# An attention and PReLU MLP kernel: batch 0's remainder rows move to the GpSimd queue, and the first two blocks of the MLP are put in another order

## The chip, the cores and the metric

The kernel runs on one core of one Trainium2 chip. The metric is device time in microseconds (us) of that core. Engines are named as in the profile: PE is TensorE's matmul, PEld its weight load, DVE is VectorE, ACT is ScalarE, POOL is GpSimd, SP is SyncE. SP, ACT and POOL each also issue DMAs on a queue of their own.

## The reference

For 8 batches and 8 heads, with S = 576 tokens and 64 columns a head, the attention has no softmax; its output, with heads side by side, is the input x (4608 x 512) of a two-layer MLP with a PReLU between.

```python
kv  = einsum('bhsd,bhse->bhde', k, v)
out = einsum('bhsd,bhde->bhse', q, kv)
x   = out / sqrt(mean(out*out, axis=-1) + 1e-6) * g_norm   # -> (4608, 512)
h   = x @ w_in                                             # (4608, 2048)
y   = (maximum(h, 0) + alpha * minimum(h, 0)) @ w_out      # (4608, 512)
```

## The kernel before

**Stages.** The 4608 tokens are cut into nine blocks of 512 (w = 0 to 8). A block's x needs the attention of the batch or two that it overlaps. While block w runs its first MLP product (16 "units" u = 0 to 15, each an `m1_group` of four matmuls into one PSUM bank), the same loop (lines 680 to 709) also runs the second product of block w-1 and the attention steps of block w+1. Block 0 is different: its first product stands alone (lines 575 to 587), its second product is written as four ordinary tiles `ys[0..3]` of 16 matmuls each (`y_run`, `y_mm`, line 353; the argument g = 0 to 15 is the depth slice), and block 1's attention is woven between them by hand (lines 598 to 640). From the second product of block 1 on (line 476, `prod_mm`), a seven-product scheme with 112 half-width matmuls a block is used; it needs sums of weights (`w_sum`) and of activations (`s_sum`), both on DVE. The prediction calls lines 598 to 640 the hand-woven part, and the loop's passes w = 1 and w = 2 loop stage 1 and loop stage 2.

**Order.** Every engine runs its instructions in the order in which the code emits them (`manual_schedule`). So a place in the code is a place in the queue of each engine that the step uses.

**The head.** Each batch has 512 "main" rows and 64 remainder rows a head. For batch 0, SP and ACT load the fp32 remainders of q, k and v into `rem0` tiles (`early_rem`, line 76) and the fp32 first four heads of q and k (`early_half`, line 82); `cast_rem` (line 534) and `cast_pair` (line 528) convert them to fp16 on DVE and ACT. POOL's queue, which converts while it loads, brings the other halves (`load_main`, line 142), then the weights and the later batches (`load_rem` line 148, `load_main`). A POOL load reuses the semaphore of the load eight places ahead of it, and waits for that one to land.

**Attention steps of a pair of heads j.** `step_t` (five transposes of q, then a copy out of PSUM, on ACT from batch 1 on, line 258), `step_kv` (five matmuls, then a masked copy on DVE, line 272), `step_ot` (line 286, squares on ACT, line 292), `ssq_mm` (line 302, `rstd` on ACT, line 304) and `norm` (`xt` on DVE, line 312). `regroup` (line 159) and `regroup_pair` (line 157) bring a batch's q and k from the staging tile into the layout of the matmuls.

**A unit.** `m1_group` takes the next PSUM bank from `h_tags`, four matmuls fill it (line 328), ACT makes `m_sb` (line 335), DVE makes `gt` from `m_sb` and the bank (line 339); only then is the bank free. In loop stage 1 there are two banks, h1 and h2, since h0 and y still hold the open tiles 2 and 3.

```python
def h_bank(name="h_ps"):
    tags = h_tags[0]
    h_turn[0] = (h_turn[0] + 1) % len(tags)
    return ps_h.tile([P, W], FP32, name=name, tag=tags[h_turn[0]])
```

PSUM banks: h0, h1, h2, y, s, q and two o (`ot`). The loop's second product takes y, h0 and q for its three accumulators.

Of the kernel before, what the change touches and what calls it, by code (L numbers as in the profile page):

```python
# [9 lines left out]
FP32 = mybir.dt.float32  # L10
# [7 lines left out]
def kernel(  # L18
# [17 lines left out]
    P = 128  # L36
    NPAIR = H // 2
# [3 lines left out]
    TPP = S // P  # L41
# [26 lines left out]
    )  # L68

    srcs = {"q": q, "k": k, "v": v}  # L70
    rem0 = {}
    st32 = {}

    def early_rem(eng, nm):
        rem0[nm] = ysb_p.tile([P, H, D], FP32, name=f"rem0{nm}", tag="y_sb")
        eng.dma_start(
            out=rem0[nm][0:REM], in_=srcs[nm][0, :, MAIN:S, :].rearrange("h s d -> s h d"),
        )

    def early_half(eng, nm, tag):  # L80
        st32[nm] = w_p.tile([P, H // 2, TPP * D], FP32, name=f"{nm}32", tag=tag)
# [2 lines left out]
            in_=srcs[nm][0, 0 : H // 2, 0:MAIN, :].rearrange("h (p t) d -> p h (t d)", t=TPP),  # L84
        )

    early_rem(nc.sync, "q")
    early_rem(nc.scalar, "k")
    early_half(nc.sync, "q", "wsum2")
    early_half(nc.scalar, "k", "wsum4")  # L90
    early_rem(nc.sync, "v")

    _set_id = list(get_activation_tables(nc.m.arch).keys()).index(
        "abs_reciprocal_sqrt_and_small"
# [32 lines left out]
    bufs = []  # L127
# [9 lines left out]
    def load_main(b, nm, h0, h1):  # L137
        st = stages.get((b, nm))
        if st is None:
            st = stage_p.tile([P, H, TPP, D], FP16, name=f"{nm}st", tag=f"{nm}st")  # L140
            stages[b, nm] = st
        nc.gpsimd.dma_start(  # L142
            out=st[:, h0:h1, :, :].rearrange("p h t d -> p h (t d)"),
            in_=srcs[nm][b, h0:h1, 0:MAIN, :].rearrange("h (p t) d -> p h (t d)", t=TPP),
        )

    def load_rem(b, nm):
        nc.gpsimd.dma_start(
            out=bufs[b % NBUF][nm][0:REM, 0 if nm == "v" else TPP, :, :],
            in_=srcs[nm][b, :, MAIN:S, :].rearrange("h s d -> s h d"),  # L150
        )
# [14 lines left out]
    def regroup_pair(b, nm, j):  # L166
        regroup(b, nm, 2 * j, 2 * j + 2, nc.scalar)
# [32 lines left out]
        return w_out_sb[i][:, r, :]  # L200

    HH = H // 2
    load_main(0, "v", 0, HH)
    load_main(0, "q", HH, H)
    load_main(0, "k", HH, H)
    ident = const_p.tile([P, P], FP32, name="ident")
    make_identity(nc, ident[:])
    load_main(0, "v", HH, H)
    for i in range(len(IN_CUTS) - 1):
        load_w_in(i)  # L210
# [184 lines left out]
    def w_sum(n, i):  # L395
        sl = slice(i * GW, (i + 1) * GW)
        if n not in wsum:
            wsum[n] = w_p.tile([P, NK, HC], FP16, name=f"wsum{n}", tag=f"wsum{n}")
        if n == 1:
            nc.vector.tensor_sub(  # L400
                out=wsum[1][:, sl, :], in0=w_lo(i, HC, D_MODEL), in1=w_lo(i, 0, HC)
            )
        elif n == 2:
            nc.vector.tensor_sub(
                out=wsum[2][:, sl, :], in0=w_hi(i, HC, D_MODEL), in1=wsum[1][:, sl, :]
            )
        elif n == 4:
            nc.vector.tensor_sub(
                out=wsum[4][:, sl, :], in0=w_hi(i, 0, HC), in1=wsum[2][:, sl, :]
            )  # L410
        else:
            nc.vector.tensor_sub(
                out=wsum[3][:, sl, :], in0=w_hi(i, HC, D_MODEL), in1=w_lo(i, HC, D_MODEL),
            )
# [115 lines left out]
            in_=st[:, 2 * j : 2 * j + 2, :].rearrange("p h (t d) -> p h t d", t=TPP),  # L530
        )

    def cast_rem(nm, eng_copy):
        eng_copy(out=bufs[0][nm][0:REM, 0 if nm == "v" else TPP, :, :], in_=rem0[nm][0:REM])

    cast_pair("q", st32["q"], 0, nc.vector.tensor_copy)
    cast_rem("q", nc.vector.tensor_copy)
    cast_pair("k", st32["k"], 0, nc.scalar.copy)
    cast_rem("k", nc.scalar.copy)
    step_t(0, 0, H_POOL)  # L540
    cast_pair("q", st32["q"], 1, nc.vector.tensor_copy)
# [52 lines left out]
    def y_run(a, gs):  # L594
        for g in gs:
            y_mm(ys[a], 0, a, g)
# [4 lines left out]
    w_sum(1, 0)  # L601
    for j, pool in enumerate((S_POOL, Q_POOL, O_POOL, O_POOL)):
        step_t(1, j, pool)
    for a in (0, 1):
        y_run(a, range(4, 8))
    y_run(2, (4, 5))
    w_sum(1, 1)
    step_kv(1, 0)
    step_kv(1, 1, Q_POOL)
# [4 lines left out]
    y_run(3, (6,))  # L614
    step_ot(1, 1)
    y_run(3, (7,))
    ssq_mm(1, 0)
    norm(1, 0)
    y_run(0, (8, 9))
    ssq_mm(1, 1, Q_POOL)  # L620
    norm(1, 1)
    y_run(0, (10, 11))
    step_ot(1, 2)
    w_sum(2, 0)
    y_run(1, (8, 9))
    step_ot(1, 3)
    w_sum(4, 0)
    y_run(1, (10, 11))
    ssq_mm(1, 2)
    norm(1, 2)  # L630
    y_run(0, (12, 13))
    ssq_mm(1, 3, Q_POOL)
    norm(1, 3)
    y_run(0, (14, 15))
    y_out(ys[0], 0, 0)
    w_sum(2, 1)
    y_run(1, range(12, 16))
    y_out(ys[1], 0, 1)
    w_sum(4, 1)
    w_sum(3, 0)  # L640
    h_tags[0] = ("h1", "h2")
    h_turn[0] = 1
    LATER = [(2, 6), (2, 7)] + [(2 + i % 2, 8 + i // 2) for i in range(2 * (NF - 8))]

    S_AT = {
# [6 lines left out]
    def unit_sums(w, u):  # L652
        for back, n, k in S_AT.get(u, ()):
            if 1 <= w + back < NW:
                s_sum(w + back, n, k)
# [4 lines left out]
            ATT_AT.setdefault(3 * j + at, []).append((what, j))  # L660
    ATT_1 = {}
    for what, ats in (
        ("kv", (3, 4, 5, 6)), ("t", (6, 7, 8, 9)), ("ot", (8, 9, 11, 12)), ("ssq", (10, 11, 13, 14))
    ):
        for j, at in enumerate(ats):
            ATT_1.setdefault(at, []).append((what, j))
    ATT = {"t": step_t, "kv": step_kv, "ot": step_ot, "ssq": step_ssq}

    def attention(w, u):
        if w < NW:  # L670
            for what, j in (ATT_1 if w == 2 else ATT_AT).get(u, ()):
                if w < B or what in ("ot", "ssq"):
                    if w == 2 and what in ("kv", "ssq"):
                        (step_kv if what == "kv" else step_ssq)(w, j, Q_POOL)
                    else:
                        ATT[what](w, j)

    REG_AT = {8 + 2 * j + i: ((nm, j),) for j in range(NPAIR) for i, nm in ((0, "q"), (1, "k"))}

    for w in range(1, NW):  # L680
        if w + 2 < B:
            load_batch(w + 2)
        for u in range(NF):
            m1_group(w, G_ORDER[u])
            unit_sums(w, u)
            if w == 1 and u == 1:
                w_sum(3, 1)
            if w == 1 and u in (2, 5):
                regroup(2, "k" if u == 2 else "q", 0, H)
            if w == 1 and u == 14:  # L690
                regroup(3, "k", 0, H)
            if w > 2 and u == 0:
                y_read(w - 2, "c12")
            if w == 1:
                for _ in range(2 if u < 2 else 1):
                    a, g = LATER.pop(0)
                    y_mm(ys[a], 0, a, g)
                    if g == NF - 1:
                        y_out(ys[a], 0, a)
            else:  # L700
                for i in range(u * PER, (u + 1) * PER):
                    prod_mm(w - 1, *Y_LIST[i])
                for what in Y_READS.get(u, ()):
                    y_read(w - 1, what)
            attention(w + 1, u)
            if w + 2 < B:
                for nm, j in REG_AT.get(u, ()):
                    if w > 1 or nm == "q":
                        regroup_pair(w + 2, nm, j)
    w = NW - 1  # L710
    store_engines[0] = (nc.sync, nc.scalar)
    for u in range(NF):
# [40 lines left out]
```

## Time and profile before

| | us |
|---|---|
| median of 3 runs | 306.36 |
| runs | 305.97 to 308.59 |
| the profiled execution, its own time | 306.55 |
| span of the profile in that execution | 304.8 |

The page's engine totals over the span are PE 281.4 us (92%), DVE 222.2 (73%), ACT 175.4 (58%), POOL 43.6 (14%). A PE total near the span does not say that PE is limiting everywhere: matmuls overlap, and their ends are modelled, so gaps between issues are larger than the idle time that is shown. The rows below go by stretch of time.

### The profile page before, as it was taken

How to read it: one execution, taken by the hardware profiler on the slowest of the kernel's cores; microseconds unless marked ns; L12 is line 12 of the kernel's file. 1: busy time of each engine (PE TensorE's matmuls, PEld its weight loads, DVE VectorE, ACT ScalarE, POOL GpSimd, SP SyncE). 2: the span in 40 equal slices, each digit the busy share in tenths (PEclk: the TensorE clock that was granted, in tenths of full speed). 3: DMA queues.
4: the chain of work that ended last, by engine and by line, in shares of the span. 5: the costliest groups of instructions: out<-in, count | busy, mean ns of one | idle time of the engine just before them, and what ended most of it. 6: DMA issues, size and time to landing. Idle time of an engine off the chain costs nothing.

```text
span 304.8 us, 5163 instructions
## 1 busy us (share of the span) xinstructions
PE 281.4 (92%) x1970; PEld 179.7 (59%) x1970; DVE 222.2 (73%) x421; ACT 175.4 (58%) x305; POOL 43.6 (14%) x61
## 2 busy tenths in 40 slices
PE   4379999897899999999999999999999999999993
PEld 1144454353476667676766676666666666666682
DVE  4256856876767887788778877887788788877861
ACT  1246736468856875687578757875664565443210
POOL 8344345240200420042003000000000000000000
PEclk9579999999999999999999999999999999999998
DMA  7999999999260398139812910021102010201223
GB/s 140 219 205 197 198 201 191 217 183 142 75 73 19 54 182 121 29 48 188 112 34 28 188 38 21 17 70 36 37 0 71 34 36 12 74 19 35 69 76 100
DMA packets 53081, 28.86 MB, mean 95 GB/s; under 512 B 15152, under 2 KB 52544, under 8 KB 53056
## 3 DMA queue, kind: packets, MB, share of 16 engines
q0 software_dynamic: 39792, 17.63, 46.2%
q1 hardware_dynamic: 11424, 9.58, 11.0%
q10 hardware_dynamic: 1840, 1.31, 1.5%
q8 instruction: 15, 0.25, 0.3%
q14 instruction: 10, 0.08, 0.1%
HBM read 36.71 MB, written 9.44 MB: 151 GB/s over the span
## 4 chain that ended last, share of the span: by engine, by line
PE 75%; DVE 10%; ACT 7%; DMA 3%; issue 3%; SPq 0%; DVEq 0%; ACTq 0%
PE h_ps L328 33%; PE yY L476 12%; PE yZ L476 10%; PE yX L476 9%; DMA q<-in_q_dram 3%; PE qt_ps L246 3%; PE kv_ps L264 3%; DVE gt L339 3%; ACT m_sb L335 3%; DVE xt L312 2%; PE ot_ps L286 2%; PE ssq_ps L302 2%; PE y L353 2%; ACT rstd L304 1%; DVE y_sb L503 1%
## 5 line engine op out<-in xcount | busy, mean ns | idle before, releaser
L328 PE MATMUL h_ps<-xt,w_in_sb 128*128 128x512 f16 x576 | 145.8, 379 | 2.1 <-DVE gt L339 1.4
L339 DVE SCALAR_TENSOR_TENSOR gt<-m_sb,beta_sb,h_ps 128x512 f16<-128x512 f32 x144 | 107.2, 747 | 51.7 <-ACT m_sb L335 49.9
L335 ACT ACTIVATE m_sb<-h_ps 128x512 f32<-128x512 f32 x144 | 86.1, 599 | 69.2 <-PE h_ps L328 53.6
L328 PEld LDWEIGHTS <-w_in_sb 128*128 128x128 f16 x576 | 54.2, 98 | 47.6 <-issue 3.8
L476 PEld LDWEIGHTS <-s 128*128 128x128 f16 x512 | 50.1, 98 | 21.6 <-issue 2.5
L476 PEld LDWEIGHTS <-gt 128*128 128x128 f16 x384 | 37.6, 98 | 15.4 <-issue 0.7
L476 PE MATMUL yY<-wsum,s 128*128 128x256 f16 x256 | 36.3, 273 | 0.0
L476 PE MATMUL yX<-w_out_sb,gt 128*128 128x256 f16 x256 | 35.1, 272 | 0.0
L292 ACT ACTIVATE sq_sb<-ot_ps 128x512 f16<-128x512 f32 x36 | 21.3, 598 | 16.8 <-PE ot_ps L286 16.4
L312 DVE SCALAR_TENSOR_TENSOR xt<-ot_ps,g2col,rstd 128x512 f16<-128x512 f32 x36 | 26.5, 746 | 5.2 <-ACT rstd L304 5.0
L304 ACT ACTIVATE rstd<-ssq_ps,eps_t 128x512 f32<-128x512 f32 x36 | 24.4, 688 | 9.8 <-PE ssq_ps L302 9.8
L258 ACT COPY qt_sb<-qt_ps 128x576 f16<-128x576 f16 x28 | 17.5, 638 | 6.4 <-PE qt_ps L246 6.4
L246 PE MATMUL qt_ps<-ident,qsb 128*128 128x128 f16 x160 | 14.5, 230 | 7.0 <-DVE qsb L528 7.0
L476 PE MATMUL yZ<-w_out_sb,s 128*128 128x256 f16 x128 | 17.5, 272 | 1.2 <-DVE y_sb L503 1.2
L353 PE MATMUL y<-w_out_sb,gt 128*128 128x512 f16 x64 | 18.4, 379 | 0.1
L142 POOL DMA_DIRECT2D vst<-in_v_dram x9 | 7.8, 869 | 68.3 <-PE kv_ps L264 62.1
L476 PE MATMUL yZ<-wsum,s 128*128 128x256 f16 x128 | 17.6, 273 | 0.0
L476 PE MATMUL yY<-wsum,gt 128*128 128x256 f16 x128 | 17.6, 273 | 0.0
L246 PEld LDWEIGHTS <-qsb 128*128 128x128 f16 x160 | 11.5, 103 | 9.8 <-DVE qsb L528 7.8
L286 PE MATMUL ot_ps<-qt_sb,kv_sb 128*128 128x512 f16 (+7 forms) x64 | 13.9, 293 | 2.6 <-DVE xt L312 2.2
L264 PEld LDWEIGHTS <-ksb 128*128 128x128 f16 x160 | 11.7, 101 | 5.6 <-issue 2.5
L264 PE MATMUL kv_ps<-vst,ksb 128*128 128x128 f16 x128 | 12.4, 224 | 2.4 <-ACT rstd L304 1.0
(60 smaller groups left out, 223.8 us busy)
## 6 DMA issues: line engine op xcount, KB each, us to landing
out_dram<-y_sb SPq DMA_DIRECT2D x72, 64.0 KB, 2.2
kst<-in_k_dram POOLq DMA_DIRECT2D x7, 512.0 KB, 9.4
qst<-in_q_dram POOLq DMA_DIRECT2D x7, 512.0 KB, 8.7
vst<-in_v_dram POOLq DMA_DIRECT2D x7, 512.0 KB, 7.1
out_dram<-y_sb SPq DMA_DIRECT2D x23, 128.0 KB, 2.1
w_out_sb<-in_moe_w_out_dram POOLq DMA_DIRECT2D x4, 512.0 KB, 16.3
w_in_sb<-in_moe_w_in_dram POOLq DMA_DIRECT2D x3, 512.0 KB, 16.1
out_dram<-y_sb SPq DMA_DIRECT2D x4, 256.0 KB, 5.2
```

The source lines that it names most:

```text
L246: nc.tensor.matmul(out=qt_ps[:, t * P : (t + 1) * P], lhsT=qs(t), rhs=ident16[:], is_transpose=True, start=(t == 0), stop=(t == NT - 1),)
L258: nc.scalar.copy(out=qts[b, j][:], in_=qt_ps[:, 0:S])
L264: nc.tensor.matmul(out=kv_ps[:], lhsT=ks(t), rhs=vs(t), start=(t == 0), stop=(t == NT - 1),)
L286: nc.tensor.matmul(out=ot_ps[:, n0 - w * W : n1 - w * W], lhsT=kvs[b, j][:], rhs=qts[b, j][:, n0 - b * S : n1 - b * S], start=True, stop=True,
L292: nc.scalar.activation(out=sq[:], in_=ot_ps[:], func=AF.Square)
L304: nc.scalar.activation(out=rstd[:], in_=ssq_ps[:], func=AF.Abs_reciprocal_sqrt, bias=eps_t[:], scale=inv_d,)
L312: nc.vector.scalar_tensor_tensor(out=xts[w, j][:], in0=ot_ps[:], scalar=g2col[:], in1=rstd[:], op0=ALU.mult, op1=ALU.mult,)
L328: nc.tensor.matmul(out=h_ps[:], lhsT=w_in_blk(c, g), rhs=xts[w, c][:], start=(c == 0), stop=(c == NC - 1),)
L335: nc.scalar.activation(out=m_sb[:], in_=h_ps[:], func=AF.Relu, scale=-1.0)
L339: nc.vector.scalar_tensor_tensor(out=gts[w, i][:, r, :], in0=m_sb[:], scalar=beta_sb[:, g : g + 1], in1=h_ps[:], op0=ALU.mult, op1=ALU.add,)
L353: nc.tensor.matmul(out=y[:], lhsT=gt_cols(w, g, a * P, (a + 1) * P), rhs=w_out_blk(g), start=(g == 0), stop=(g == NF - 1),)
L476: nc.tensor.matmul(out=bank, lhsT=lhs, rhs=rhs, start=fresh, stop=(c == NK - 1), skip_group_check=True,)
```

## The change

1. `early_rem`, `cast_rem` and the `rem0` tiles are gone. SP's and ACT's queues begin with the fp32 halves of q and k. POOL's queue begins with the three remainders of batch 0 (`load_rem(0, ...)`), converted while they load; `ident` is made ahead of the last half of k.
2. In the hand-woven part, tiles 2, 0 and 1 are all finished (48 matmuls, with the 8 of tile 3 that stood there already); before, tiles 0 and 1 were. Weight sums and batch 2's k copy move ahead of the loop.
3. In loop stage 1 only the last 8 matmuls of tile 3 are left, and h_tags has three banks until the first unit of loop stage 2 has taken its bank.
4. Attention steps of block 2 take other units and, in part, other banks: kv alternates q and o, the third `ot` takes y. Copies of batch 3's q move to units 12 to 15; its k moves from one DVE copy to four ACT copies in units 0 and 1 of loop stage 2. The first `s_sum`s move by a unit.

```diff
-    early_rem(nc.sync, "q")
-    early_rem(nc.scalar, "k")
     early_half(nc.sync, "q", "wsum2")
     early_half(nc.scalar, "k", "wsum4")
-    early_rem(nc.sync, "v")
...
     HH = H // 2
+    for nm in ("q", "k", "v"):
+        load_rem(0, nm)
     load_main(0, "v", 0, HH)
     load_main(0, "q", HH, H)
-    load_main(0, "k", HH, H)
     ident = const_p.tile([P, P], FP32, name="ident")
     make_identity(nc, ident[:])
+    load_main(0, "k", HH, H)
...
-    for a in (0, 1):
+    for a in (2, 0, 1):
         y_run(a, range(4, 8))
-    y_run(2, (4, 5))
...
+    y_run(2, (8,))
     ssq_mm(1, 0)
     norm(1, 0)
-    y_run(0, (8, 9))
+    y_run(2, (9, 10))
     ssq_mm(1, 1, Q_POOL)
     norm(1, 1)
-    y_run(0, (10, 11))
+    w_sum(2, 0)
+    w_sum(4, 0)
+    y_run(2, (11,))
+    y_run(0, (8, 9, 10))
     step_ot(1, 2)
...
     norm(1, 3)
-    y_run(0, (14, 15))
+    regroup(2, "k", 0, H)
+    w_sum(4, 1)
+    w_sum(3, 0)
+    w_sum(3, 1)
+    y_run(0, (13, 14, 15))
     y_out(ys[0], 0, 0)
-    w_sum(2, 1)
+    y_run(2, range(12, 16))
+    y_out(ys[2], 0, 2)
     y_run(1, range(12, 16))
     y_out(ys[1], 0, 1)
...
-    h_tags[0] = ("h1", "h2")
-    h_turn[0] = 1
+    h_turn[0] = 0
+    h_tags[0] = ("h0", "h1", "h2")
...
-        ("kv", (3, 4, 5, 6)), ("t", (6, 7, 8, 9)), ("ot", (8, 9, 11, 12)), ("ssq", (10, 11, 13, 14))
+        ("kv", (1, 2, 3, 4)), ("t", (5, 6, 7, 9)), ("ot", (7, 8, 10, 11)), ("ssq", (9, 10, 12, 13))
...
+                        pool = O_POOL if what == "kv" and j % 2 else Q_POOL
+                    elif w == 2 and what == "ot" and j == 2:
+                        step_ot(w, j, (ps_y, "y"))
...
+    REG_1 = {12 + j: (("q", j),) for j in range(NPAIR)}
...
+            if w == 1 and u == 4:
+                regroup(2, "q", 0, H)
+            if w == 2 and u == 0:
+                h_tags[0] = ("h1", "h2")
...
+            if w == 2 and u < 2:
+                for j in (2 * u, 2 * u + 1):
+                    regroup_pair(3, "k", j)
```

POOL's queue at the start, before. vst, qst and kst are the staging tiles of v, q and k; the shapes are partitions x heads x elements.

```order
L142 DMA vst<-in_v_dram 128x4x256
L142 DMA qst<-in_q_dram 128x4x256
L142 DMA kst<-in_k_dram 128x4x256
masks.py:197 MEMSET ident 128x128
masks.py:199 ISA
masks.py:199 AFFINE_SELECT ident<-ident 128x128
L142 DMA vst<-in_v_dram 128x4x256
L180 DMA w_in_sb_158<-in_moe_w_in_dram 128x4x256
```

POOL's queue at the same place after the change; qsb, ksb and vsb are the fp16 tiles that the matmuls read.

```order
L138 DMA qsb_126<-in_q_dram 64x8x64
L138 DMA ksb_122<-in_k_dram 64x8x64
L138 DMA vsb_124<-in_v_dram 64x8x64
L132 DMA vst<-in_v_dram 128x4x256
L132 DMA qst<-in_q_dram 128x4x256
masks.py:197 MEMSET ident 128x128
masks.py:199 ISA
masks.py:199 AFFINE_SELECT ident<-ident 128x128
L132 DMA kst<-in_k_dram 128x4x256
L132 DMA vst<-in_v_dram 128x4x256
L170 DMA w_in_sb_155<-in_moe_w_in_dram 128x4x256
```

Three loads now stand ahead of all others on POOL's queue, and every later load is three places further back.

DVE's queue from the third and fourth `norm` of block 1 into loop stage 1, before (wsum are the weight sums, ksb_140 is batch 2's k).

```order
L312 SCALAR_TENSOR_TENSOR xt<-ot_ps,g2col,rstd 128x512 x2
L404 TENSOR_TENSOR wsum_598<-w_out_sb_183,wsum_486 128x1024
L408 TENSOR_TENSOR wsum_607<-w_out_sb_183,wsum_598 128x1024
L412 TENSOR_TENSOR wsum_639<-w_out_sb_181,w_out_sb_171 128x1024
L339 SCALAR_TENSOR_TENSOR gt<-m_sb,beta_sb,h_ps 128x512 x2
L412 TENSOR_TENSOR wsum_639<-w_out_sb_183,w_out_sb_176 128x1024
L339 SCALAR_TENSOR_TENSOR gt<-m_sb,beta_sb,h_ps 128x512
L159 COPY ksb_140<-kst 128x8x4x64
```

The same place after; batch 2's k is ksb_134 here.

```order
L304 SCALAR_TENSOR_TENSOR xt<-ot_ps,g2col,rstd 128x512 x2
L149 COPY ksb_134<-kst 128x8x4x64
L400 TENSOR_TENSOR wsum_590<-w_out_sb_180,wsum_588 128x1024
L404 TENSOR_TENSOR wsum_627<-w_out_sb_178,w_out_sb_168 128x1024
L404 TENSOR_TENSOR wsum_627<-w_out_sb_180,w_out_sb_173 128x1024
L331 SCALAR_TENSOR_TENSOR gt<-m_sb,beta_sb,h_ps 128x512 x2
L264 TENSOR_TENSOR kv_sb<-kv_ps,mask_109 128x128
```

The copy of batch 2's k has moved from behind the third `gt` of loop stage 1 to ahead of the first, and no weight sum is left between `gt`s.

ACT's queue at the end of loop stage 1 and the start of loop stage 2 after the change (qsb_126 and ksb_122 are batch 3's q and k).

```order
L296 ACTIVATE rstd<-ssq_ps,eps_t 128x512
L147 COPY qsb_126<-qst 128x2x4x64
L327 ACTIVATE m_sb<-h_ps 128x512
L147 COPY qsb_126<-qst 128x2x4x64
L327 ACTIVATE m_sb<-h_ps 128x512
L147 COPY qsb_126<-qst 128x2x4x64
L327 ACTIVATE m_sb<-h_ps 128x512
L250 COPY qt_sb<-qt_ps 128x576
L147 COPY ksb_122<-kst 128x2x4x64 x2
L327 ACTIVATE m_sb<-h_ps 128x512
L147 COPY ksb_122<-kst 128x2x4x64 x2
L327 ACTIVATE m_sb<-h_ps 128x512
```

The four q copies now stand in the last four units, and four k copies have come in behind them.

## Rows read from the trace of the kernel before

**Rows 1.** The page: its first line, and DMA's busy tenths in 40 slices.
```profile
span 304.8 us, 5163 instructions
DMA  7999999999260398139812910021102010201223
```
**Rows 2.** Windows by stretch: us, PE, PEld, DVE, ACT, POOL busy (instructions), clock, DMA share, GB/s.
```profile
0.00:12.00 12.00, 3.68 (x10) 1.23 (x10) 4.23 (x18) 2.17 (x3) 7.52 (x15) 0.85 0.92 176
12.00:24.65 12.65, 9.43 (x56) 5.34 (x57) 6.38 (x17) 6.11 (x11) 5.38 (x7) 0.74 1.35 201
38.00:53.40 15.40, 14.74 (x100) 7.59 (x98) 8.71 (x16) 8.10 (x15) 7.44 (x10) 1.00 1.48 196
53.40:83.00 29.60, 25.05 (x152) 12.51 (x151) 22.13 (x39) 19.84 (x36) 6.75 (x9) 1.00 1.13 157
83.00:113.50 30.50, 30.25 (x232) 20.62 (x230) 23.50 (x45) 21.43 (x38) 4.09 (x6) 1.00 0.60 81
```
**Rows 3.** Timeline of the head: start us, us, engine, line, operation [idle before, releaser].
```profile
0.74 0.76 SPq L76 DMA_DIRECT2D rem0q<-in_q_dram  x1
1.56 0.85 SPq L82 DMA_DIRECT2D q<-in_q_dram  x1
...
11.53 0.43 DVE L528 CAST qsb<-q 128x512 f16<-128x512 f32 x1 [6.51 <-DMA q<-in_q_dram]
...
12.01 0.71 PE L246 MATMUL qt_ps<-ident,qsb 128*128 128x128 f16 x5 [6.12 <-DVE qsb L528]
...
13.70 0.62 ACT L534 CAST vsb<-rem0v 64x512 f16<-64x512 f32 x1 [0.93 <-DMA rem0v<-in_v_dram]
...
15.66 0.58 PE L264 MATMUL kv_ps<-vst,ksb 128*128 128x128 f16 x4
```
**Rows 4.** DMA queues from 5 to 9 us (packets, MB), and q's issue (KB, us to landing).
```profile
q0 software_dynamic: 430, 0.21, 40.9%
q1 hardware_dynamic: 383, 0.39, 36.0%
q10 hardware_dynamic: 434, 0.44, 35.5%
...
q<-in_q_dram SPq DMA_DIRECT2D x1, 512.0 KB, 9.9
```
**Rows 5.** Timeline of POOL's queue: what each issue waited for.
```profile
35.21 0.69 POOL L148 DMA_DIRECT2D vsb<-in_v_dram  x1 [1.93 <-DMA qst<-in_q_dram]
...
40.79 0.88 POOL L142 DMA_DIRECT2D qst<-in_q_dram  x1 [1.12 <-DMA vst<-in_v_dram]
...
49.21 0.88 POOL L142 DMA_DIRECT2D vst<-in_v_dram  x1 [1.50 <-PE ssq_ps L302]
```
**Rows 6.** Waits of PE from 53.4 to 83 us: total us, times, longest.
```profile
PE ot_ps L286 <- DVE xt L312: 1.7, 2, 0.9
PE h_ps L328 <- DVE gt L339: 1.1, 2, 0.9
PE kv_ps L264 <- DVE ksb L159: 0.8, 1, 0.8
PE h_ps L328 <- DVE xt L312: 0.5, 1, 0.5
```
**Rows 7.** Timeline of PE in the hand-woven part.
```profile
49.66 0.38 PE L286 MATMUL ot_ps<-qt_sb,kv_sb 128*128 128x64 f16 x2 [0.48 <-DVE xt L312]
```
**Rows 8.** Windows, columns as in rows 2: late in loop stage 1.
```profile
70.00:80.00 10.00, 7.90 (x37) 3.35 (x36) 7.40 (x13) 8.91 (x18) 0.00 (x0) 1.00 0.72 83
```
**Rows 9.** The chain of waits: start us, us that the piece adds, what.
```profile
42.00 1.12 PE qt_ps L246 x20
43.11 2.16 PE y L353 x10
...
83.14 0.86 PE h_ps L328 x4
84.00 0.76 PE yX L476 x7
```
**Rows 10.** Windows, columns as in rows 2: the clock around PE's first pause.
```profile
8.00:10.00 2.00, 0.00 (x0) 0.00 (x0) 0.00 (x0) 0.00 (x0) 0.50 (x1) 0.60 1.23 271
10.00:18.00 8.00, 5.05 (x29) 2.97 (x30) 2.92 (x8) 2.89 (x6) 3.30 (x5) 0.50 1.41 197
18.00:20.00 2.00, 1.45 (x12) 1.02 (x11) 1.41 (x4) 1.40 (x3) 0.88 (x1) 0.84 1.23 205
```

More of the change, by code (lines that the diff above doesn't have):

```diff
@@ L70 @@
     srcs = {"q": q, "k": k, "v": v}
-    rem0 = {}
     st32 = {}
[L74 to L78, printed above, removed]
     def early_half(eng, nm, tag):
@@ L531, in cast_pair @@
         )
-    def cast_rem(nm, eng_copy):
-        eng_copy(out=bufs[0][nm][0:REM, 0 if nm == "v" else TPP, :, :], in_=rem0[nm][0:REM])
     cast_pair("q", st32["q"], 0, nc.vector.tensor_copy)
-    cast_rem("q", nc.vector.tensor_copy)
     cast_pair("k", st32["k"], 0, nc.scalar.copy)
-    cast_rem("k", nc.scalar.copy)
     step_t(0, 0, H_POOL)
@@ L542 @@
     cast_pair("k", st32["k"], 1, nc.scalar.copy)
-    cast_rem("v", nc.scalar.copy)
     step_t(0, 1, H_POOL)
@@ L616 @@
     y_run(3, (7,))
+    y_run(2, (8,))
     ssq_mm(1, 0)
     norm(1, 0)
-    y_run(0, (8, 9))
+    y_run(2, (9, 10))
     ssq_mm(1, 1, Q_POOL)
     norm(1, 1)
-    y_run(0, (10, 11))
+    w_sum(2, 0)
+    w_sum(4, 0)
+    y_run(2, (11,))
+    y_run(0, (8, 9, 10))
     step_ot(1, 2)
-    w_sum(2, 0)
-    y_run(1, (8, 9))
+    y_run(0, (11,))
+    y_run(1, (8,))
     step_ot(1, 3)
-    w_sum(4, 0)
-    y_run(1, (10, 11))
+    y_run(1, (9, 10))
     ssq_mm(1, 2)
+    w_sum(2, 1)
     norm(1, 2)
-    y_run(0, (12, 13))
+    y_run(1, (11,))
+    y_run(0, (12,))
     ssq_mm(1, 3, Q_POOL)
     norm(1, 3)
-    y_run(0, (14, 15))
+    regroup(2, "k", 0, H)
[3 more added lines that the diff above has]
+    y_run(0, (13, 14, 15))
     y_out(ys[0], 0, 0)
-    w_sum(2, 1)
+    y_run(2, range(12, 16))
+    y_out(ys[2], 0, 2)
     y_run(1, range(12, 16))
     y_out(ys[1], 0, 1)
-    w_sum(4, 1)
-    w_sum(3, 0)
-    h_tags[0] = ("h1", "h2")
-    h_turn[0] = 1
-    LATER = [(2, 6), (2, 7)] + [(2 + i % 2, 8 + i // 2) for i in range(2 * (NF - 8))]
+    h_turn[0] = 0
+    h_tags[0] = ("h0", "h1", "h2")
     S_AT = {
@@ L673, in attention @@
                     if w == 2 and what in ("kv", "ssq"):
-                        (step_kv if what == "kv" else step_ssq)(w, j, Q_POOL)
+                        pool = O_POOL if what == "kv" and j % 2 else Q_POOL
+                        (step_kv if what == "kv" else step_ssq)(w, j, pool)
+                    elif w == 2 and what == "ot" and j == 2:
+                        step_ot(w, j, (ps_y, "y"))
                     else:
                         ATT[what](w, j)
+    REG_1 = {12 + j: (("q", j),) for j in range(NPAIR)}
     REG_AT = {8 + 2 * j + i: ((nm, j),) for j in range(NPAIR) for i, nm in ((0, "q"), (1, "k"))}
@@ L684 @@
             m1_group(w, G_ORDER[u])
[L685 to L691, printed above, removed]
+            if w > 1:
+                unit_sums(w, u)
+            if w == 1 and u == 4:
+                regroup(2, "q", 0, H)
+            if w == 2 and u == 0:
+                h_tags[0] = ("h1", "h2")
             if w > 2 and u == 0:
@@ L694 @@
             if w == 1:
[L695 to L699, printed above, removed]
+                if u < NF // 2:
+                    y_mm(ys[3], 0, 3, NF // 2 + u)
+                    if u == NF // 2 - 1:
+                        y_out(ys[3], 0, 3)
             else:
@@ L705 @@
             attention(w + 1, u)
+            if w == 1:
+                for k in {7: (0,), 9: (1,), 13: (2,)}.get(u, ()):
+                    s_sum(1, 1, k)
+                    s_sum(1, 2, k)
             if w + 2 < B:
-                for nm, j in REG_AT.get(u, ()):
-                    if w > 1 or nm == "q":
-                        regroup_pair(w + 2, nm, j)
+                for nm, j in (REG_1 if w == 1 else REG_AT).get(u, ()):
+                    regroup_pair(w + 2, nm, j)
+            if w == 2 and u < 2:
+                for j in (2 * u, 2 * u + 1):
+                    regroup_pair(3, "k", j)
     w = NW - 1
```

## The prediction

> **What bounds the kernel now.** I read the windows by stretch first [rows 2]. From 83 to 113.5 us, one loop stage in steady state, PE is busy 30.25 of 30.5 us: from there on PE is the bound, the change alters nothing in those stages, and a microsecond saved earlier comes out at the end. Before 83 us PE is not the bound. It is busy 3.68 of the first 12 us, 9.43 of the next 12.65, and 25.05 of the 29.6 us of loop stage 1. So I look at three places: the start, the hand-woven part, loop stage 1. The page [rows 1] adds that the DMA engines are full for about the first ten slices, 76 us; any change of loads must be asked whether it delays what stands behind.
>
> *The start.* The timeline [rows 3] shows PE's first transposes at 12.01 us, behind DVE's conversion of q at 11.53, behind the load of q, issued at 1.56 behind the remainder's load at 0.74. That load took 9.9 us to land [rows 4]. The DMA queues from 5 to 9 us show why: POOL's queue (q0), SP's (q1) and ACT's (q10) get 430, 383 and 434 packets, equal shares, so q's half goes at a third of the packet rate.
>
> *Loop stage 1.* PE's own waits [rows 6] are 1.7 us for an `ot` bank until `xt` is made, 1.1 us for an h bank until `gt` is made, 0.8 us for k's copy and 0.5 us for `xt` of block 2; the gaps between issues are longer than these idles, since a matmul's end is modelled. ACT holds 8.91 us of 18 instructions in 70 to 80 us, 0.495 us each [rows 8]: it is close behind PE there.
>
> **The change part by part.** The sum is made against the profiled execution, 306.55 us (span 304.8, 1.75 around it); the median of the runs, 306.36, is 0.2 lower.
>
> *Queue heads.* Without `rem0`, q's half is issued at 0.74 instead of 1.56, and does not stand behind 512 small packets of its own queue. The rival for packets is now the remainders on POOL's queue instead of half of v. Bounds for the landing (11.51 before). The earlier start alone: the issue moves by 0.82 us, and up to as much again falls away with the packets no longer ahead, so 0.8 to 1.6; I use 1.3, if q's packet rate stays at 383 in 4 us. At the other end POOL's packets are so small that q and k have the engines to themselves: their 1024 packets, at the 1247 in 4 us that three queues moved together, take 3.3 us, where q's 512 at its share take 5.3. That is 2.0 us less, with the 1.3 a shift of 3.3. I take 2.3, the middle. The following steps wait on each other, so they shift with q: the transposes, v's remainder (the cast at 13.70 goes, but kv at 15.66 did not wait for it, PE was in its warm-up matmuls), kv, `ot`, norms. Removing the casts of the remainders, 0.41 us on DVE and twice 0.6 on ACT, is worth nothing beyond that, since q's conversion and the transposes hide it.
>
> Do the loads keep up? POOL waits for the load eight places ahead, so its issues show landings [rows 5]: batch 1's q by 35.2 us, its v by 40.8, batch 2's k by 49.2. They are wanted at 39.97, 45.1 and 58.7 us now, and, with the shift, at about 37.5, 43 and 51. They hold, by about 2 us each. What the small packets of 128 B cost POOL's queue is not in these rows. Below, it is their bytes, 64 KB at 197 GB/s or 0.33 us each, 1 us for three; above, each packet costs what the mean one of rows 4 does, 4 us over 1247 or 3.2 ns, so 1.6 us for 512 and 5 for three, of which the same rows taken off SP and ACT give back part. The rows read from memory are the same in number and size as before, so I take zero, and keep up to 2 us late as a loss.
>
> The Trainium skill (DMA: Bandwidth & Descriptors, Specifications) names 512 B as the least transfer for full rate, with a read-modify-write below; the remainders' 128 B pieces fall under it, where 256 B pieces did too. No row here prices it, and by it the sum would lie nearer the upper bound just given, some 302 us. The same page (Issuing engines are not separate DMA queues) has all queues on the same 16 engines, interleaved; the equal packet counts in rows 4 agree, and by this alone the shift would come from order, not from added bandwidth, as I have it.
>
> *Hand-woven part.* Ten more matmuls stand here, ten fewer in loop stage 1: 2.16 us [rows 9] moved, nothing gained. As cover they count: `ot` of pair 2 waited 0.48 us for `xt` [rows 7], and shorter gaps lie around the two `ssq`s behind it. Between that `ssq` and that `ot` stand 8 matmuls of block 0 after the change, 6 before, so 0.43 us more cover; the later gaps get one or two more each. I take 1.1 us, out of bounds 0 and 1.5. PE busy is 14.74 of 15.4 [rows 2], that is 0.66 of plain idle, and each gap hides another 0.16 of a modelled end. The three weight sums and the k copy put ahead of the loop cost DVE 2.5 us between `xt` and the first `gt`; PE has 11 matmuls, 2.4 us, and then a unit, 0.86 us, before that `gt` is wanted. If k were late, DVE would stand there and every `gt` behind it.
>
> *Loop stage 1, up to the second unit of loop stage 2.* Before: 53.41 to 82.97 us, 29.56, less the 2.16 moved out: 27.4 for like work. After, PE's own work is 16 units at 0.86 [rows 9], 8 matmuls of tile 3 at 0.22, four pairs at 0.28 (t), 0.28 (kv), 0.22 (ot), 0.22 (ssq): 19.5; with the first unit of loop stage 2, its seven products 0.76 and five transposes 0.28: 21.4. To this I add what the new order still makes wait. (a) q's copy on DVE in unit 4 stands behind that unit's `gt` and ahead of kv's copy; the transposes of unit 5 come 0.55 us too early. (b) ssq takes the one q bank at units 9, 10, 12 and 13, so the second of each two waits for the `rstd` of the first: 0.6 and 0.4. (c) ACT has 28 instructions from unit 5 to 15, 13.9 us at 0.495, and PE 13.0: ACT ends about one unit late, so `gt` does. (d) h_turn: seventeen calls from 0 end on index 2, h2; then the list becomes two long and (2+1)%2 is 1, h2 again. The second unit of loop stage 2 waits for the `gt` of the unit just before it. With (c) I make that 1.55 us; without either it would be none. (e) 0.2 at the first banks. In sum 21.4+0.55+1.0+1.55+0.2 = 24.7, a gain of 2.7. Bounds: PE alone, 21.4, a gain of 6; or ACT and DVE as late as before, no gain. The `ot` waits of 1.7 and the wait for k, 0.8, are gone in either, the third `ot` in y and k ahead of the loop. The four k copies on ACT in loop stage 2, 2 us, are hidden: ACT is busy 21.4 of 30.5 us there.
>
> *Sum.* 2.3 + 1.1 + 2.7 = 6.1; 306.55 - 6.1 = 300.5 us. About 1% is what a measurement of this kernel can tell from no change.
>
> **The rivals.** *The head gives nothing:* remainders share the engines packet for packet and hold q or the v behind them, or loads further on are late by the 2.3 gained. For it: the equal shares in rows 4, and margins of only 2 us. Against it: q has fewer packets ahead. Time: 306.55 - 3.8 = 302.8. *Loop stage 1 does not shorten:* ACT, behind by a unit, and h2 taken twice eat the 2.7; 303.2. For it: rows 8; against it: three banks allow a unit of lag. *Neither:* the order is changed but each wait only moves on: 306. *Slower, by the clock:* PE's clock reads 0.60 in 8 to 10 us, 0.50 to 18 and 0.84 to 20 [rows 10]: after the warm-up matmuls it falls to the lower of its two levels, 1.2 GHz, and comes back at about 18.6 us, PE having resumed at 12.01 and gone from step to step. If, with other gaps, it stayed low into block 0's first product, each us at half speed would cost about 0.5; it is slower than before once the low level lasts 12 us longer, to about 28 us, and at 35 us the time would be 310. Against it: the steps from the transposes on are the same and as dense. The Trainium skill (TensorE: Matmul & The Clock Gate, Part 1) says that activity releases the throttle, which is what 12 to 18.6 us shows.
>
> **How the numbers follow.** Forecast (both gains, 297.8 to 303) 0.62; head nothing 0.15; stage nothing 0.12; neither 0.06; slower 0.05. Range 297.8 to 304.0: below it are the 3.3 shift and 3 us more of the stage's bound; above it lie neither, slower, and half of one single loss. Faster by over 1% (under 303.3): the forecast, nearly all of the first rival and a little of the second, 0.78; within 1% the rest of these and neither, 0.16; slower 0.06.
>
> **What would show it.** First transposes at about 9.7 us, kv at 13.3; loop stage 1's first unit at about 52, the second unit of loop stage 2 near 77; no `ot` wait for `xt` in the stage; one wait for a `gt` at that second unit. Wrong if q lands after 10.5, if DVE stands for batch 2's k at 51 us, or if ACT is over 95% busy through the last six units.

## The result, and the profile after

The changed kernel takes 297.93 us (median of 4 runs, 297.52 to 298.45) where the kernel before takes 306.54 beside it: a ratio of 0.9707, 95% interval 0.9666 to 0.9749. A second set on another chip gives 297.63 (6 runs) and 0.9698 (0.9665 to 0.9731). Of the 306.36 us that the prediction started from, 0.9707 is 297.4 us: faster, as forecast, but by 9 us and not by 6, just under the low end of the range, 297.8.

The page after, its first line and DMA's tenths, against [rows 1]:

```profile
span 295.8 us, 5159 instructions
DMA  7999999999631990199019401110103011201223
```

The windows after (columns as in [rows 2]): the first 12 us; the two stretches of the head that matter below; the last units of loop stage 1; the stretch from the first unit of loop stage 1 to the second of loop stage 2; one steady stage.

```profile
0.00:12.00 12.00, 8.47 (x34) 3.68 (x34) 6.21 (x23) 2.44 (x4) 9.62 (x19) 1.00 1.02 168
...
6.00:8.00 2.00, 1.22 (x7) 0.45 (x5) 1.19 (x3) 1.14 (x2) 2.00 (x4) 1.00 0.97 64
...
10.00:18.00 8.00, 5.20 (x41) 3.10 (x41) 4.28 (x11) 3.78 (x7) 4.80 (x7) 1.00 1.40 199
...
62.00:74.00 12.00, 9.95 (x58) 5.03 (x57) 10.76 (x19) 11.95 (x24) 1.56 (x2) 1.00 1.54 202
...
49.17:74.20 25.03, 22.08 (x141) 11.58 (x140) 20.32 (x36) 19.75 (x37) 7.31 (x10) 1.00 1.52 208
...
83.00:113.50 30.50, 30.25 (x232) 20.65 (x230) 24.00 (x45) 21.52 (x39) 4.71 (x6) 1.00 0.66 94
```

PE does 8.47 us of work in the first 12 us, where it did 3.68. The steady stage is the same to the hundredth. The timeline of the head after, against [rows 3]:

```profile
0.74 0.45 SPq L75 DMA_DIRECT2D q<-in_q_dram  x1
...
1.25 0.82 POOL L138 DMA_DIRECT2D qsb<-in_q_dram  x1 [0.80 <-POOLq L737]
...
5.83 0.61 DVE L520 CAST qsb<-q 128x512 f16<-128x512 f32 x1
...
6.50 0.71 PE L238 MATMUL qt_ps<-ident,qsb 128*128 128x128 f16 x5
...
10.47 0.58 PE L256 MATMUL kv_ps<-vst,ksb 128*128 128x128 f16 x4 [0.38 <-DMA vst<-in_v_dram]
```

The first transposes come at 6.50 us, not at 12.01. Five points of PE's timeline, each the same step in both kernels, say where the 9 us are:

| step | before | after | earlier by |
|---|---|---|---|
| first transposes | 12.01 | 6.50 | 5.51 |
| first matmul of block 0's first product | 23.41 | 17.93 | 5.48 |
| first matmul of the y tiles | 38.08 | 32.60 | 5.48 |
| first unit of loop stage 1 (before: + 2.16 of matmuls that moved ahead of it) | 55.57 | 49.17 | 6.40 |
| second unit of loop stage 2 | 82.97 | 74.20 | 8.77 |
| end of the span | 304.8 | 295.8 | 9.0 |

So in these two traces the head is worth 5.5 us, the hand-woven part 0.9, loop stage 1 2.4, and another 0.2 comes behind that stretch. The 5.5 is one pair of heads, and heads vary from run to run (first experiment and last section).

PE's own waits after, from 45 to 100 us (total us, times, longest), against [rows 6]:

```profile
PE h_ps L320 <- DVE gt L331: 1.5, 1, 1.5
PE ssq_ps L294 <- ACT rstd L296: 0.7, 2, 0.6
PE qt_ps L238 <- DVE qsb L149: 0.7, 1, 0.7
PE yZ L468 <- DVE y_sb L495: 0.2, 1, 0.2
```

The `ot` waits and the wait for k are gone; q's copy, the two waits of ssq and one wait for `gt` have come, as (a), (b) and (c, d) of the forecast had them.

### The profile page after: what moved, and what is told of

Read it like the earlier page. It is cut to its first block, busy times and chain, and to the rows that moved or that the text cites. A ratio compares the mean times of both kernels' runs of the same rounds, so it can differ in the third digit from the quotient of the medians.

```text
span 295.8 us, 5159 instructions
## 1 busy us (share of the span) xinstructions
PE 280.1 (95%) x1970; PEld 179.3 (61%) x1970; DVE 221.5 (75%) x419; ACT 176.1 (60%) x307; POOL 45.9 (16%) x64
## 4 chain that ended last, share of the span: by engine, by line
PE 69%; DMA 18%; ACT 5%; issue 3%; DVE 2%; POOL 1%; DVEq 0%; POOLq 0%; ACTq 0%
PE h_ps L320 31%; PE yY L468 12%; PE yZ L468 10%; PE yX L468 9%; DMA qst<-in_q_dram 6%; DMA vst<-in_v_dram 5%; DMA w_in_sb<-in_moe_w_in_dram 5%; DMA ksb<-in_k_dram 2%; ACT m_sb L327 2%; PE qt_ps L238 2%; PE ssq_ps L294 2%; PE kv_ps L256 2%; PE ot_ps L278 2%; DVE y_sb L495 1%; ACT ksb L147 1%
## 5 line engine op out<-in xcount | busy, mean ns | idle before, releaser
L345 PE MATMUL y<-w_out_sb,gt 128*128 128x512 f16 x64 | 17.1, 379 | 0.1
L294 PE MATMUL ssq_ps<-sq_sb,mask 128*128 128x512 f16 x36 | 13.5, 379 | 1.4 <-ACT rstd L296 0.7
L238 PEld LDWEIGHTS <-qsb 128*128 128x128 f16 x160 | 10.9, 100 | 5.2 <-DVE qsb L520 1.9
```

What stands on the lines that cost most here:

```text
L238: nc.tensor.matmul(out=qt_ps[:, t * P : (t + 1) * P], lhsT=qs(t), rhs=ident16[:], is_transpose=True, start=(t == 0), stop=(t == NT - 1),)
```

## Experiments

Kernels named together were timed on one chip beside the kernel before. The first four are about where the gain of the head comes from.

### The head alone, and the blocks alone

The first takes the kernel before and gives it only point 1 of the change. The second takes the changed kernel and gives it back the old head.

```diff
# head alone, on the kernel before
-    early_rem(nc.sync, "q")
-    early_rem(nc.scalar, "k")
...
-    early_rem(nc.sync, "v")
+    for nm in ("q", "k", "v"):
+        load_rem(0, nm)
...
```

> The kernel before with the change of the head alone (queues of SP, ACT and POOL for batch 0, casts). The trace after has block 0's first product 5.48 us earlier (17.93 against 23.41 us); if the later stages follow, the time is 306.5 - 5.5 = 301.0 us. Rival: my forecast's 2.3 us for the head, the rest of the gain coming from the blocks: 304.2 us. Second rival: the loads of batches 1 and 2, no earlier than before, stop the shift in the hand-woven part: 303 us or more, with DVE waiting for k or q of batch 2.

> The changed kernel with the head of the kernel before. If head and blocks add up, this gains what e1_head_only leaves of the whole, 8.8 - 5.5 = 3.3 us: 303.2 us, loop stage 1 and the first unit of loop stage 2 taking the same 25 us as in the changed kernel. Rival: the blocks gain more than that when the loads have 5.5 us more to arrive (batch 2's q was waited for in the changed kernel): 302.5 us. Other rival: they bring their gain only with the early head: 306 us.

Head alone: 302.51 us, 0.9847 (0.9807 to 0.9888), 4.2 us less than the 306.75 of before there. Blocks alone: 302.70, 0.9853 (0.9810 to 0.9896), 4.05 less. Together that is 8.3, where the whole change brings 8.6 (306.54 to 297.93). But with the head alone, loop stage 1 began at 47.34 us, 6.1 earlier than before; a quarter of that was gone by the end (span 300.2, 4.6 less than before's). The time of 301.0 that was expected if the later stages follow did not come. Its timeline, PE and ACT late in loop stage 1 (qst is the staging tile of batch 3's q here):

```profile
64.56 0.62 ACT L147 COPY qsb<-qst 128x512 f16<-128x512 f16 x1 [1.53 <-DMA qst<-in_q_dram]
...
66.50 1.02 PE L320 MATMUL h_ps<-xt,w_in_sb 128*128 128x512 f16 x4 [1.56 <-DVE gt L331]
```

ACT stands 1.53 us for a load, the `m_sb` behind that copy is late, so `gt` is, and PE waits 1.56. The load stream did not move forward with the head. The old order asks for this q at about 63 us; in the changed kernel the four copies come from 68.5 us on and wait for no load.

The blocks alone come near the rival's 302.5, but not by its way: in their trace the hand-woven part gains 0.8 us, and the stretch from the first unit of loop stage 1 to the second of loop stage 2 takes 24.83 us, a gain of 2.6, so 3.3 as in the table; that q is there in time brings at most the 0.2 by which this stretch is below 25.03. The rest of the 4.05 lies in the head. This kernel has the old head, and its first product starts 1.26 us earlier than the 23.41 of the kernel before:

```profile
22.15 1.02 PE L328 MATMUL h_ps<-xt,w_in_sb 128*128 128x512 f16 x4
```

So the old head takes 22.15 or 23.41 us by chance, and the new one between 16.95 and 18.26, in the seven traces that have it as it stands. By the pairs of traces the new head is worth 3.9 to 6.5 us. By the times it is worth 4.2 us on the old blocks, where a part is lost again, and 4.5 on the new ones (0.9853 less 0.9707, of 306.36).

### What in the head does it: the order on POOL's queue, or on SP's and ACT's

The first kernel is the changed one with v's half ahead of the remainders on POOL's queue. The second keeps fp32 remainders on SP and ACT, but behind the halves, and POOL's queue as it was before.

```diff
# v's half first, on the changed kernel
+    load_main(0, "v", 0, HH)
     for nm in ("q", "k", "v"):
         load_rem(0, nm)
-    load_main(0, "v", 0, HH)
# remainders behind, on the changed kernel with the old head
-    early_rem(nc.sync, "q")
-    early_rem(nc.scalar, "k")
     early_half(nc.sync, "q", "wsum2")
     early_half(nc.scalar, "k", "wsum4")
+    early_rem(nc.sync, "q")
+    early_rem(nc.scalar, "k")
     early_rem(nc.sync, "v")
```

> The changed kernel with the first half of v ahead of the three remainders on POOL's queue, as before the change; SP's and ACT's queues as after. Theory A (q and k had the engines to themselves, because POOL's first load, a remainder, moved no packet before 5 us): v's packets start at about 3 us and take a third, q lands at about 8 instead of 5.8, and the time is about 2 us longer, 299.8 us. Rival C (packets of SP's and ACT's queues hold POOL's off, whatever POOL's first load is): v starts at about 5 us too, q lands at 5.8, and the time is 297.5 us or a little less, since v is there sooner.

> The changed kernel, but batch 0's remainders stay in fp32 on SP's and ACT's queues with their casts, only behind the halves of q and k instead of ahead; POOL's queue as before the change. Rival B (all that counted is that q and k no longer stand behind remainders on their own queues): q lands at about 6 us and the time is 297.5 us or less. Theory A (a POOL queue that begins with v shares from 3 us): q lands at about 8 us, and the time is about 300 us.

They took 299.83 us (0.9748, 0.9696 to 0.9800) and 300.48 (0.979, 0.9745 to 0.9835). PE's timeline with v's half first:

```profile
6.54 0.40 PE L238 MATMUL qt_ps<-ident,qsb 128*128 128x128 f16 x4
9.61 0.23 PE L238 MATMUL qt_ps<-ident,qsb 128*128 128x128 f16 x1 [2.67 <-DMA qsb<-in_q_dram]
```

And DVE and PE with the remainders behind:

```profile
5.84 0.43 DVE L528 CAST qsb<-q 128x512 f16<-128x512 f32 x1 [0.83 <-DMA q<-in_q_dram]
...
9.95 0.29 PE L246 MATMUL qt_ps<-ident,qsb 128*128 128x128 f16 x1 [3.23 <-DVE qsb L534]
```

In all three kernels q's half is there at 5.8 us, whatever stands first on POOL's queue. So it is the order on SP's and ACT's queues that brings it. With v's half first, the time is that of theory A, but q landed when rival C has it: POOL's packets began only at 5.2 us there too. But a pair's fifth transpose needs the remainder, and that comes 3 us later in these two: kv starts at 12.78 and 13.18 us, not at 10.47. The remainders at the front of POOL's queue are what makes the early half usable.

How the half gets so early shows in the packets of q0 (POOL), q1 (SP) and q10 (ACT). The DMA queues before, from 3 to 4 and from 4 to 5 us:

```profile
q1 hardware_dynamic: 500, 0.12, 55.4%
q0 software_dynamic: 78, 0.04, 38.0%
q10 hardware_dynamic: 68, 0.02, 7.6%
...
q0 software_dynamic: 171, 0.09, 82.9%
q10 hardware_dynamic: 33, 0.03, 13.8%
q1 hardware_dynamic: 6, 0.01, 4.6%
```

The same after, from 3 to 4 and from 4 to 5 us:

```profile
q1 hardware_dynamic: 180, 0.18, 52.0%
q10 hardware_dynamic: 146, 0.15, 44.2%
...
q10 hardware_dynamic: 224, 0.23, 66.2%
q1 hardware_dynamic: 150, 0.14, 41.5%
```

Before, from 3 to 4 us SP sends the remainder's packets of 256 B; of q's half, issued at 1.56, hardly a packet has gone by 5 us, and then the three queues share [rows 4]. Why it does not begin at 4 us, when the remainder's packets have gone, no run shows. After, packets of 1 KB flow from 2 us on, on two queues, while POOL's queue sends none before 5 us, although its first load was issued at 1.25.

### Is POOL's queue held off until the others are done?

The changed kernel, with both fp32 halves loaded twice.

```diff
     early_half(nc.sync, "q", "wsum2")
     early_half(nc.scalar, "k", "wsum4")
+    q32, k32 = st32["q"], st32["k"]
+    early_half(nc.sync, "q", "wsum1")    # second copies, read by nobody
+    early_half(nc.scalar, "k", "wsum3")
+    st32["q"], st32["k"] = q32, k32
```

> The changed kernel, with the fp32 halves of q and k loaded a second time by SP and ACT, right behind the first, into tiles that nobody reads (work is added, none left out). In the changed kernel the two halves land at 5.8 us and POOL's first packets come at 5.0 us. Theory: packets of POOL's queue do not start while the two other queues still have such rows; then POOL's first packets come only at 7.3 to 8 us, q's remainder lands at 9 to 10 instead of about 6.8, the fifth transpose waits for it, kv comes at about 13 and the time is about 300.5. Rival: POOL's queue starts at 5.0 us whatever the others do; then three queues share from there, q's remainder lands at 7.5 to 8.5, and the time is 298.5 to 299.5. In both the first transposes stay at 6.5 us.

300.72 us, 0.9833 (0.9809 to 0.9858). Its DMA queues, from 5.5 to 6 and from 7 to 7.5 us, and PE's fifth transpose:

```profile
q1 hardware_dynamic: 104, 0.11, 64.2%
q10 hardware_dynamic: 68, 0.07, 37.2%
q0 software_dynamic: 17, 0.00, 6.6%
...
q1 hardware_dynamic: 74, 0.08, 54.6%
q10 hardware_dynamic: 74, 0.08, 42.5%
q0 software_dynamic: 71, 0.01, 27.5%
```

```profile
10.04 0.29 PE L242 MATMUL qt_ps<-ident,qsb 128*128 128x128 f16 x1 [3.47 <-DMA qsb<-in_q_dram]
```

Neither theory holds whole. POOL's first packets come in this window and not at 5.0, so the start is not fixed; but they come while both other queues still have rows, so POOL is not held off until these are done. From there the shares are equal, 74, 74 and 71 packets, which is why q's remainder takes until 10 us. The time follows the theory's number (300.5), for the rival's reason in part. What delays POOL's first packets stays open: they came 2 us after the issue before, nearly 4 after the change, 4.4 here.

### The waits of loop stage 1

The first kernel is the changed one with one line more, term (d): the second unit of loop stage 2 takes h1. The second has that line, ssq in two banks in turn (term b), and seven of batch 3's eight copies moved from the last four units of loop stage 1 and units 0 and 1 of loop stage 2 to units 0 to 8 of loop stage 2 (term c).

```diff
                 h_tags[0] = ("h1", "h2")
+                h_turn[0] = 1
# in the second kernel also
-                        pool = O_POOL if what == "kv" and j % 2 else Q_POOL
+                        if j % 2:
+                            pool = O_POOL if what == "kv" else S_POOL
+                        else:
+                            pool = Q_POOL
...
-    REG_1 = {12 + j: (("q", j),) for j in range(NPAIR)}
+    REG_1 = {14: (("q", 0),)}
+    REG_2 = {0: (("k", 0),), 1: (("q", 1),), 2: (("k", 1),), 4: (("q", 2),), ...}
...
```

> The changed kernel with one line more: h_turn[0] = 1 where h_tags goes back to two banks, so that the second unit of loop stage 2 takes h1 instead of h2 a second time. In the changed kernel this unit waits 1.50 us for gt at 74.20 us. If the bank taken twice is most of that wait (term (d) of the sum), the unit waits at most 0.8 us, for the gt of one unit further back, and the time falls by about 0.8 us, to some 297.2. If ACT being a unit late is all of it (term (c)), the bank does not matter: the wait stays at 1.5 and the time at 297.9.

> The same line, and two changes against the other waits of loop stage 1: ssq of block 2 alternates the banks q and s, so that no ssq waits for the rstd before it (0.56 and 0.19 us in the changed kernel), and of batch 3's eight copies on ACT only one stays in loop stage 1 (unit 14), the other seven go to units 0, 1, 2, 4, 5, 7 and 8 of loop stage 2, so that ACT is not a unit late at its end. Theory: the three waits of 1.50, 0.56 and 0.19 us go, and the time falls by 1.5 to 2.3 us, to 295.6 to 296.4. Rival: the copies that are moved make ACT late in loop stage 2, or batch 3's transposes wait for q there, and the waits only move on: 297 to 298.

297.15 us (0.971, 0.9686 to 0.9733) and 297.24 (0.9714, 0.9694 to 0.9734), too close to the changed kernel to tell from times. The trace tells more. In the first, the wait of that unit falls from 1.50 to 0.69 us, and the stretch from 25.03 to 24.01 (from 50.18 to 74.19). It started 1.0 us late because in its profiled run the clock was granted at 0.72 from 10 to 18 us and 0.92 from 18 to 33; in the changed kernel it reads 1.00 in both. So the changed kernel and the one with the line were timed once more, side by side on one chip:

> The changed kernel itself, once more, beside the one with the line h_turn[0] = 1, on the same chip. Its median before was 297.93 us; expected 297.3 to 298.2.

> The changed kernel with the line h_turn[0] = 1, beside the changed kernel on the same chip. Its trace had the stretch from the first unit of loop stage 1 to the second of loop stage 2 at 24.01 us, where the changed kernel has 25.03, but its profiled run lost 1 us between the head and the first y tile, with the clock granted at half there. Theory: 0.7 to 1.0 us faster than the changed kernel, 296.5 to 297.2. Rival: what the trace showed was given back elsewhere, within 0.3 us of it.

The changed kernel takes 297.63 us (297.20 to 298.83), with the line 296.86 (296.44 to 297.47; 0.9668 of before, 0.9639 to 0.9697). That is 0.77 us less, as (d) has it. The intervals against before overlap, so the times alone would not carry it; the wait in the trace does. PE with the line, second unit of loop stage 2:

```profile
73.03 1.02 PE L320 MATMUL h_ps<-xt,w_in_sb 128*128 128x512 f16 x4 [0.69 <-DVE gt L331]
```

The second kernel says more about (b) and (c). All its waits of PE from 60 to 80 us, and the windows from 62 to 78 us of the changed kernel and of this one:

```profile
PE h_ps L320 <- DVE gt L331: 0.7, 1, 0.7
```

```profile
62.00:78.00 16.00, 13.75 (x87) 7.61 (x86) 12.73 (x24) 15.33 (x30) 2.38 (x3) 1.00 1.27 162
...
62.00:78.00 16.00, 15.02 (x91) 8.03 (x90) 13.54 (x25) 13.69 (x27) 1.56 (x2) 1.00 1.26 162
```

The ssq waits are gone and ACT, with 13.69 us of 16, is no longer full (15.33 in the changed kernel). Yet the stretch takes 24.05 us, as with the one line alone (24.01), and the wait at that unit is the same 0.69. So ACT's load was not behind that wait. The starts of PE's groups say where ssq's gain went: with the one line there are gaps of 0.72 and 0.36 us ahead of the two ssq, with the second kernel five gaps of 0.13 to 0.29 us between 64 and 71.6 us (before two ssq, an `ot` and two units), 1.07 us in all, as much as before.

DVE, which neither kernel relieved, is the likely reason. In the second kernel it works without a listed wait from 65.14 to 74.5 us; the window, and the timeline ahead of that unit:

```profile
65.14:74.50 9.36, 8.38 (x46) 4.03 (x44) 9.22 (x16) 7.87 (x15) 0.00 (x0) 1.00 1.53 203
...
71.21 0.42 DVE L418 TENSOR_TENSOR s<-gt 128x512 f16<-128x512 f16 x1
71.66 0.43 DVE L420 TENSOR_TENSOR s<-s,gt 128x512 f16<-128x512 f16 x1
72.00 2.21 DVE L331 SCALAR_TENSOR_TENSOR gt<-m_sb,beta_sb,h_ps 128x512 f16<-128x512 f32 x3
```

ACT had the `m_sb` of the last two units of loop stage 1 ready at 70.4 and 71.4 us, but an `xt` and two `s_sum`s stood ahead of their `gt`s on DVE. The second of these three `gt`s frees h1, and PE goes on at 73.45. With h2 taken twice it is the third that PE waits for, 0.74 us more, which is term (d). This is read from the trace: no kernel moved DVE's work.

### Do block 0's stores hold up batch 2's q?

The changed kernel without the stores of tiles 2, 0 and 1 of block 0: these rows of the output are not written.

```diff
-        store_rows(w * W + a * P, y_sb[:], 0, D_MODEL)
+        if a == 3:
+            store_rows(w * W + a * P, y_sb[:], 0, D_MODEL)
```

> The changed kernel without the stores of block 0's tiles 2, 0 and 1 (those rows of the output are not written; tile 3's are). In the changed kernel they leave at 47 to 50 us, 0.75 MB, while batch 2's q is on its way, and q lands 16.8 us after its issue, at 56.85 us, just as DVE is done with the gt ahead of its copy (56.77). Theory: the stores make it 2 us late, and this costs nothing yet: q lands at 54.5 to 55.5 us, the transposes of unit 5 still wait 0.6 to 0.7 us, because the copy stands behind that gt, and the time stays within 0.3 us of 297.9. Rival: the stores do not slow the load, which stays at 56.8. Second rival: the load stream bounds the stage, and the time falls by 1 us or more.

297.24 us, 0.9713 (0.9695 to 0.9732) where the changed kernel has 0.9707: the same time. The issue of batch 2's q (KB each, us to landing) after, and then without the stores:

```profile
qst<-in_q_dram POOLq DMA_DIRECT2D x1, 512.0 KB, 16.8
```

```profile
qst<-in_q_dram POOLq DMA_DIRECT2D x1, 512.0 KB, 14.2
```

The stores cost this load 2.6 us (with them it takes 16.2 to 17.3 us in five traces), and the kernel 0.2 at most (49.02 to 73.84 us is 24.82). The reason is that q lands just when it is wanted. In the second run of the changed kernel the head was 0.85 us quicker still, loop stage 1 began at 48.32, and DVE then had to wait for it:

```profile
56.66 0.69 DVE L149 COPY qsb<-qst 128x2048 f16<-128x2048 f16 x1 [0.32 <-DMA qst<-in_q_dram]
```

Kv had waited 0.3 us for v before that, and the second unit of loop stage 2 came at 73.98, only 0.22 earlier. Loads now cap what the head can still give.

## Why the prediction was wrong, and where it was right

**The queue heads, 2.3 us, measured 5.5 (and no less than 3.9 in any pair of traces): this step failed.** The bounds were 1.3 and 3.3, and both counted too little. The start: I let q gain the 0.82 us of its earlier issue and as much again for the packets ahead. But q's half, issued at 1.56 before, had sent at most 6 packets by 5 us, and it sends from 2 us on after the change: nearly 3 us. I had read the queues from 5 to 9 us only [rows 4], where all three are at work, and took from there that the half had been waiting on its share all along; the rows from 3 to 5 us would have shown that it had not begun. The rate: the upper end, engines for q and k alone, was the true one, and in full: 512 packets take some 3.5 us from 2 us on, where they took over 6 from 5 us on. I took the middle and did not ask when POOL's packets would start. Before, they started at 3.3 us; after, at 5, when q's half was nearly through. The kernel with the remainders behind shows that the order on SP's and ACT's queues brings all of this by itself.

**The remainders' small packets, taken as zero, cost something where I did not look.** From 6 to 8 us the DMA engines move 64 GB/s, against 199 from 10 to 18 us. A pause is part of that (21 GB/s from 6.5 to 7.1 us), and the second run has 108 there; but from 6 to 6.5 us POOL's small packets have the engines nearly to themselves:

```profile
q0 software_dynamic: 236, 0.03, 93.2%
```

That is 32 ns of an engine for a packet of 128 B. SP's packets of 256 B took 18 ns before (500 at 55.4% of 1 us, above). By these, as an estimate, the 1536 packets of the three remainders take all 16 engines 3.1 us where they took 1.7, inside the prediction's bounds of 1 and 5. v's half stands behind them, and kv waits 0.38 us for it (0.63 in the second run, 1.06 with the line for h1); the gain of the head at kv is 5.2, not 5.5, and PE makes it up behind that. The trace agrees with the Trainium skill (DMA: Bandwidth & Descriptors, Specifications), which has 512 B as the least size for full rate; the 302 us to which the sum came by that rule did not come.

**Do the loads keep up: right for 2.3 us, used up at 5.5.** The prediction gave the loads a margin of 2 us each. After, batch 2's q lands 16.75 us after its issue at 40.10, at 56.85, and the `gt` ahead of its copy ends at 56.77. The three tiles whose stores now leave together before it had not been counted as a price on that load; they are 2.6 us of it.

**Hand-woven part, 1.1, measured 0.9; loop stage 1, 2.7, measured 2.4.** Both mechanisms hold, and so do the parts that can be seen: q's copy 0.70 (0.55 in the sum), ssq 0.56 and 0.19 (0.6 and 0.4), the second unit of loop stage 2 1.50 (1.55). Of this last one, the bank taken twice is 0.8 us. But I explained the rest by ACT being a unit late, and that explanation falls: with ACT relieved the wait is still 0.69. DVE, which the trace shows behind it, is not in the sum of that wait. And the parts do not add as the sum had them: with ssq's 0.75 away nothing came out at the end. That the total was nearly right is in part luck.

**The signs named in advance.** The first transposes came at 6.50 us and kv at 10.47, not at 9.7 and 13.3. The first unit of loop stage 1 and the second of loop stage 2 came at 49.2 and 74.2, not at 52 and 77: by the 3.2 us that the head was mis-sized, less 0.2 for the hand-woven part and, for the second, 0.3 more for loop stage 1. "ACT over 95% busy through the last six units" came true (11.95 of 12 us) and meant nothing: the instructions overlap, and relieving ACT changed no time. That criterion was badly chosen. The rivals: none came. The clock did not stay low for longer: after the change kv's matmuls run at the lower pace (0.58 us), but the ten transposes behind the first `ot` take 0.73 us, where they took 1.19 before, so full speed was back before them. What this gives is taken back by kv's wait for v and a longer wait of the next `ot`s, and the step from the first transposes to block 0's first product takes 11.43 us, as before (11.40). So in this pair of traces the clock nets to nothing in the 5.5 us.

## What to carry to other kernels

To see what a load at the front waits for, read its queue from its issue to its first packet, and not only where all queues are busy: here the half of q was late by its start as much as by its share. What is first needed goes first on the queue of the engine that can issue first, and what completes it goes to the front of another queue, or the early landing buys nothing. When a head gets shorter by several us, ask again of every load behind it whether it still lands in time, stores on the same engines included.

## What the runs showed of the hardware that I had not expected

A queue can be silent for long after an issue: POOL's first packets came 2 us after its first issue with small packets on the other queues, nearly 4 us with rows of 1 KB on both, whether a remainder or v's half stood first, and 4.4 with twice as many of these rows. Once it runs beside two busy queues, its share of the packets is equal to theirs (74, 74, 71 in 0.5 us). The Trainium skill (DMA: Bandwidth & Descriptors, Issuing engines are not separate DMA queues) has the transfers of all engines interleave on the same 16 DMA engines, and the trace agrees; that section says nothing of the silence before.

The same kernel, profiled twice, had its first product of block 0 start at 17.93 and 16.95 us, and with the line for h1, which touches nothing ahead of 70 us, at 18.26 and 17.37. The granted clock from 10 to 18 us reads 0.72 in the third of these four and 1.00 in the others. But a reading of 1.00 is not always full pace: in the first run of the changed kernel kv's first four matmuls took 0.58 us, as they did under a granted 0.50 before [rows 3, 10], in its second run, also under 1.00, 0.38:

```profile
9.95 0.38 PE L256 MATMUL kv_ps<-vst,ksb 128*128 128x128 f16 x4 [0.63 <-DMA vst<-in_v_dram]
```

So up to 1.3 us of a trace's head can be chance (the old head had its two starts as far apart), the length of the same small matmuls shows it better than the clock's row, and a change of less than that is better read from a stretch that starts behind it. In that first run the trace's record of the clock begins only at 11.5 us, behind these matmuls, which is why the row has nothing but 1.00 there.
